# Which engines normalize the fourth group of token blocks: two blocks on VectorE, one on GpSimd and one on ScalarE, in place of four on GpSimd

## The chip, the cores and the metric

The kernel runs on one core of one Trainium2 chip. The metric is device time in microseconds (us) of one execution; the value given is the median of the runs, with the lowest and the highest beside it. A profile is one further execution, recorded instruction by instruction, with a time of its own.

Five engines matter here. TensorE (PE in the profile) multiplies matrices; VectorE (DVE), ScalarE (ACT) and GpSimd (POOL) work elementwise; SyncE (SP) does no arithmetic and issues the transfers (DMA). Each takes its instructions in one fixed order, and an instruction that waits holds up those behind it on its engine.

## The reference

Two branches are computed from the same normalized input and summed with it. The layer norm `xn` of `x` (2048 tokens of 448 channels) comes first:

```
def reference(A_x, A_w_r, A_w_i, B_x, B_w1, B_w2, B_w3, B_w4):
    x = A_x
    xn = _layernorm(x, axis=-1)
    return x + _A_ref(xn, A_w_r, A_w_i) + _B_ref(xn, B_w1, B_w2, B_w3, B_w4)
```

Branch A is a spectral filter: a two-dimensional real FFT, a product with complex weights, and the inverse. Branch B is a mixer:

```
h = _gelu(_layernorm(x, axis=-1) @ w1)
...
hs = jnp.concatenate([g0, g1, g2, g3], axis=-1) @ w2
x1 = x + hs
h2 = _gelu(_layernorm(x1, axis=-1) @ w3) @ w4
return x1 + h2
```

The input of `@ w1` is thus normalized twice. `g0` to `g3` are the four quarters of the channels of `h`, shifted by +1, -1, +2 and -2 tokens.

## The kernel before

**Tiles.** The tokens are cut into 16 blocks of 128 partitions by 448 channels in float32; `xb(b)` is block b, part of a tile `xt`. Neighbouring tokens lie in different blocks, so a shift by tokens is mostly a change of block. Four blocks make a group, and `GRP[3]` is blocks 10, 11, 12 and 13. Values that enter a matmul are split into a high and a low half in float16, and products are made of three matmuls (high by high, low by high, high by low).

**The first stage, group by group.** `norm1(g, apply)` takes the statistics of a group's four blocks on VectorE (L306, L307), makes a first estimate of the reciprocal root (L324 to L327) and the product with the mean (L328, tile `nma`), and then normalizes each block in place: one multiply-add for each block with a scale and a bias for each partition, on the engine that the list `apply` names (L333 on ScalarE, L336 on VectorE or GpSimd). It gives back `refine`, some ten small GpSimd operations (L343 to L352) that finish the root; the last makes `gsc`, the scale that the GELU of that group needs. `scales` (L360 to L367) makes from it the correction `cs` (L365), by which `w2_tile` needs to multiply a block. `refine` and `scales` run on GpSimd alone.

A group then needs its transposed copy `xT`. Groups 0 to 2 are transposed on TensorE (L389) and split by ScalarE and VectorE (L393, L394). Group 3 goes through `turn(3)`: for each block ScalarE copies the high half (L866), VectorE subtracts it twice to get the low half (L867 for 64 channels, L868 for 384), and SyncE issues a transposing DMA (L869).

**`w1_unit(g, i)`** multiplies block i of group g with `w1` (11 matmuls, L420), applies GELU (L460) and writes the high (L461) and low half (L464) into the shift buffer in `x2mem`. When the neighbours of a block are all done, SyncE issues the transposing DMA into `hT`, tile `h` (L475): unit (2,0), block 6, releases block 4. The transposing DMAs of `turn` and those of the units share SyncE's queue.

**`w2_tile(b)`** multiplies `h` of block b with `w2` (11 matmuls, L484) into one of two PSUM banks, and VectorE adds the result to `cs` times the block (L485). With two banks, the third tile cannot begin before the first has been evicted. After L485 come the second layer norm (`ln2`), transposes of its output (L520), and the large multiplications with `w3` (L400) and `w4` (L814), which fill most of the rest of the program. The spectral branch runs between them.

**The order.** The program is not run in source order. A scheduler places the instructions on each engine by priority (by and large the order of the source) and by when it expects their inputs, and the order is then fixed in the program. `behind(key)` holds instructions behind a named earlier one on the same engine. The multiplications of `w3` and `w4` are given a late priority (`FILL`), so that they take what the others leave of TensorE.

The steps around the change, in source order:

Of the kernel before, what the change touches and what calls it, by code (L numbers as in the profile page):

```python
# [125 lines left out]
def body(tc, nc, x, wf, w1, w2, w3, w4, c_g, c_n, c_small, out):  # L126
    V, A, P, T, SY = nc.vector, nc.scalar, nc.gpsimd, nc.tensor, nc.sync
# [40 lines left out]
    def xb(b):  # L168
        return xt[b // 2][:, b % 2]
# [130 lines left out]
    def stats(src, key, mv=None, pins=None):  # L300
        if mv is None:
            mv = pc.tile([128, 4, 2], F32, tag="mv", bufs=3, name=f"mv{key}")
        for i, s in enumerate(src):
            st = pc.tile([128, 6], F32, tag="st", bufs=4, name=f"st{key}_{i}")
            with behind(*pins[i]) if pins else contextlib.nullcontext():
                V.bn_stats(out=st, in_=s)  # L306
            V.bn_aggr(out=mv[:, i, :], in_=st)  # L307
        return mv
# [10 lines left out]
    def norm1(g, apply, pins=None):  # L319

        bs, c = GRP[g], slice(4 * g, 4 * g + 4)
        mv, a, y, nm = mva[:, c], va[:, :, c], vy[:, :, c], nma[:, c]
        stats([xb(b) for b in bs], f"a{g}", mv, pins)
        V.tensor_scalar(out=a[:, 1], in0=mv[:, :, 1], scalar1=1.0 + EPS, scalar2=EPS * EPS, op0=ALU.mult, op1=ALU.add)  # L324
        V.tensor_scalar(out=a[:, 0], in0=mv[:, :, 1], scalar1=EPS, scalar2=None, op0=ALU.add)
        V.tensor_single_scalar(vyi[:, :, c], va.bitcast(I32)[:, :, c], 1, op=ALU.logical_shift_right)
        V.tensor_scalar(out=vyi[:, :, c], in0=vyi[:, :, c], scalar1=-1, scalar2=0x5F3759DF, op0=ALU.mult, op1=ALU.add)  # L327
        i = V.scalar_tensor_tensor(out=nm, in0=mv[:, :, 0], scalar=-1.0, in1=y[:, 1], op0=ALU.mult, op1=ALU.mult)  # L328
        after["c", g] = (i.ins,)
        for k, b in enumerate(bs):  # L330
            y_, m_ = y[:, 1, k:k + 1], nm[:, k:k + 1]
            if apply[k] is A:
                i = A.activation(out=xb(b), in_=xb(b), func=AF.Identity, scale=y_, bias=m_)  # L333
                after["na", g] = (i.ins,)
            else:
                i = apply[k].tensor_scalar(out=xb(b), in0=xb(b), scalar1=y_, scalar2=m_, op0=ALU.mult, op1=ALU.add)  # L336
                after["n" if apply[k] is V else "np", g] = (i.ins,)

        q, z = (pc.tile([128, 2, 4], F32, tag=f"v{t}", bufs=2, name=f"v{t}{g}") for t in "qz")
        w, r = vw[:, :, c], vr[:, :, c]  # L340

        def refine():
            P.tensor_tensor(out=q, in0=y, in1=y, op=ALU.mult)  # L343
            P.tensor_tensor(out=q, in0=q, in1=a, op=ALU.mult)
            P.tensor_scalar(out=w, in0=q, scalar1=-10.0 / 3.0, scalar2=None, op0=ALU.add)
            P.tensor_tensor(out=w, in0=w, in1=q, op=ALU.mult)
            P.tensor_scalar(out=w, in0=w, scalar1=5.0, scalar2=None, op0=ALU.add)
            P.tensor_tensor(out=z, in0=w, in1=w, op=ALU.mult)
            P.tensor_tensor(out=z, in0=z, in1=q, op=ALU.mult)
            P.tensor_scalar(out=z, in0=z, scalar1=-0.5 * 0.375 ** 3, scalar2=1.5 * 0.375, op0=ALU.mult, op1=ALU.add)  # L350
            P.tensor_tensor(out=r, in0=z, in1=w, op=ALU.mult)
            i = P.tensor_scalar(out=gsc[:, c], in0=r[:, 1], scalar1=r1, scalar2=None, op0=ALU.mult)  # L352
            after["g", g] = (i.ins,)
        return refine
# [19 lines left out]
    @contextlib.contextmanager  # L374
    def behind(*key):
        key = key if len(key) > 1 else key[0]
        with contextlib.ExitStack() as st:
            for i in after[key]:
                st.enter_context(tc.issue_after(i))
            yield  # L380
# [501 lines left out]
    n1 = [norm1(0, [P,V,P,V])]  # L882
# [90 lines left out]
    n1[2]()  # L973
    scales(0, 3)
    with behind("a2"):
        n1 = [norm1(3, [P, P, P, P])]
    for k in range(4):
        w1_unit(2, k)
    for k in range(4):
# [166 lines left out]
```

## Time and profile before

| | |
|---|---|
| median of 3 runs | 409.43 us (409.42 to 409.53) |
| profiled execution, its own time | 409.47 us |
| its span (first to last instruction) | 407.7 us |
| TensorE busy | 400.2 us (98%) |
| VectorE busy | 334.7 us (82%) |
| ScalarE busy | 254.1 us (62%) |
| GpSimd busy | 101.0 us (25%) |
| granted TensorE clock, mean | 0.998 |

Times in the profile's rows are us from the start of the span, unless marked ns. A row of a timeline has start, length, engine, line, operation, the tile written and those read (`out<-in`), partitions by elements, and a count; neighbouring instructions of one kind are merged into one row. A bracket at its end says how long the engine stood idle before it and what ended that. A row of a group has the busy time and the mean ns of one, and after the second bar the idle time before the group. A row that lists one line's instructions has their lowest, median and highest length in ns. A row of windows has the stretch, its length, then busy time and count of PE, PEld (weight loads), DVE, ACT and POOL, the granted clock, the busy share of DMA and its GB/s. "SPq" is SyncE issuing a transfer: the length is that of the issue, not of the transfer.

### The profile page before, as it was taken

What the parts mean: (1) busy time and instruction counts of PE and PEld (TensorE: products, weight loads), DVE (VectorE), ACT (ScalarE), POOL (GpSimd) and SP (SyncE); (2) the same over time, 40 slices, a digit from 0 to 9 for tenths busy, and PEclk for the clock granted to TensorE, in tenths of its full rate; (3) what the DMA queues carried; (4) which work ended last, traced back from release to release, by engine and by line L of the source; (5) the groups of instructions that cost most, each with busy time, mean ns of one, the idle gap of its engine ahead of it and who ended that gap; (6) DMA issues with size and microseconds to landing.
All of it is one profiled execution on the core that took longest, in us unless ns stands there. A gap on an engine that the chain in (4) does not pass through costs nothing.

```text
span 407.7 us, 8731 instructions
## 1 busy us (share of the span) xinstructions
PE 400.2 (98%) x3391; PEld 297.6 (73%) x3391; DVE 334.7 (82%) x704; ACT 254.1 (62%) x431; POOL 101.0 (25%) x158
## 2 busy tenths in 40 slices
PE   8999999999999999999999999999999999999995
PEld 3555455865767877777878878787677789998994
DVE  5899799999746897988698888965999999966644
ACT  4787979774468867555698878853354555452431
POOL 6759810111146956500021111110000000000000
PEclk9999999999999999999999999999999999999999
DMA  8978975666759752636256657500012023100101
GB/s 274 382 281 177 247 143 130 135 123 146 182 121 276 238 169 65 221 99 180 73 145 166 153 128 185 131 27 2 24 68 75 20 92 90 47 2 2 45 2 46
DMA packets 54597, 52.08 MB, mean 128 GB/s; under 512 B 35678, under 2 KB 48542, under 8 KB 54556
## 3 DMA queue, kind: packets, MB, share of 16 engines
q1 hardware_dynamic: 54556, 51.53, 46.4%
q8 instruction: 26, 0.43, 0.5%
q14 instruction: 15, 0.12, 0.1%
HBM read 38.28 MB, written 3.67 MB: 103 GB/s over the span
## 4 chain that ended last, share of the span: by engine, by line
PE 89%; POOL 5%; DVE 2%; ACT 1%; issue 1%; DMA 1%; POOLq 0%
PE pw L400 33%; PE acc L814 23%; PE pw L484 6%; PE side L784 4%; PE acc L784 3%; PE pu L673 3%; PE ps L573 3%; PE pe L694 2%; PE pp L628 2%; PE px L645 2%; PE py L715 2%; PE wps L844 2%; PE pw L420 2%; POOL xt L336 1%; POOL w2p L938 1%
## 5 line engine op out<-in xcount | busy, mean ns | idle before, releaser
L400 PE MATMUL pw<-x2mem,w3p 128*128 128x256 f16 x1232 | 151.5, 273 | 0.0
L400 PEld LDWEIGHTS <-w3p 128*128 128x128 f16 x1232 | 119.0, 98 | 19.5
L814 PE MATMUL acc<-w4p,hf 128*128 128x448 f16 (+1 forms) x516 | 104.3, 348 | 0.0
L814 PEld LDWEIGHTS <-hf 128*128 128x128 f16 x516 | 50.1, 98 | 37.6
L732 ACT ACTIVATE pw<-pw,pe 128x512 f32<-128x512 f32 x42 | 27.4, 653 | 27.7 <-PE pw L400 27.6
L735 DVE SCALAR_TENSOR_TENSOR hf<-pw,h,hf 128x512 f16<-128x512 f32 x42 | 31.2, 744 | 12.9 <-ACT hf L734 12.7
L484 PE MATMUL pw<-w2p,h 128*128 128x448 f16 x176 | 36.4, 352 | 1.3 <-DMA h<-x2mem 0.7
L420 PE MATMUL pw<-w1p,xT 128*128 128x448 f16 x176 | 35.0, 352 | 0.0
L654 POOL TENSOR_TENSOR z<-te 128x450 f32<-128x450 f32 x16 | 15.7, 981 | 70.8 <-DVE te L652 65.9
L734 ACT ACTIVATE hf<-pw,h 128x512 f16<-128x512 f32 x42 | 28.8, 686 | 4.2 <-PE acc L814 3.2
L484 PEld LDWEIGHTS <-h 128*128 128x128 f16 x176 | 17.1, 98 | 16.7 <-DMA h<-x2mem 1.7
L750 ACT ACTIVATE hz<-g,h 128x896 f16<-128x896 f32 x14 | 14.6, 1042 | 23.1 <-DVE g L747 23.1
L420 PEld LDWEIGHTS <-xT 128*128 128x128 f16 x176 | 17.1, 99 | 15.8 <-DVE xT L394 0.4
L784 PEld LDWEIGHTS <-hz 128*128 128x128 f16 x294 | 28.3, 98 | 0.6
L635 ACT ACTIVATE pf<-pp 64x450 f16<-64x450 f32 x32 | 17.4, 543 | 12.5 <-DVE pf L636 9.6
L636 DVE TENSOR_TENSOR pf<-pp,pf 64x450 f16<-64x450 f32 x32 | 19.9, 622 | 5.1 <-ACT pf L635 4.8
L751 DVE SCALAR_TENSOR_TENSOR hz<-g,h,hz 128x896 f16<-128x896 f32 x14 | 16.1, 1147 | 6.7 <-ACT hz L750 6.7
L556 POOL TENSOR_TENSOR f<-xr 128x452 f32<-128x452 f32 x16 | 19.7, 1250 | 0.6
L564 DVE TENSOR_TENSOR xh<-f,xh 128x452 f16<-128x452 f32 x16 | 14.3, 915 | 6.2 <-ACT xh L563 6.2
L650 ACT ACTIVATE te<-px 64x450 f32<-64x450 f32 x32 | 17.3, 540 | 1.2 <-PE px L645 0.6
L744 ACT ACTIVATE g<-pw,pe 128x512 f32<-128x512 f32 x14 | 9.6, 683 | 11.3 <-PE pw L400 11.2
L563 ACT ACTIVATE xh<-f 128x452 f16<-128x452 f32 x16 | 8.7, 573 | 9.5 <-POOL f L556 7.8
(189 smaller groups left out, 707.3 us busy)
## 6 DMA issues: line engine op xcount, KB each, us to landing
wc<-wf SPq DMA_DIRECT2D x32, 225.0 KB, 3.8
wl<-wf SPq DMA_DIRECT2D x8, 450.0 KB, 4.1
xt<-x SPq DMA_DIRECT2D x8, 448.0 KB, 7.3
xf<-x SPq DMA_DIRECT2D x8, 448.0 KB, 4.4
loads<-x SPq DMA_DIRECT2D x7, 448.0 KB, 3.9
out<-xt SPq DMA_DIRECT2D x13, 224.0 KB, 1.9
w3raw<-w SPq DMA_DIRECT2D x3, 896.0 KB, 10.9
gn<-c_g SPq DMA_DIRECT2D x16, 128.0 KB, 3.0
```

The lines of the kernel that those rows point to most:

```text
L400: T.matmul(ps_out, wp[:, wi + t, cols], xT[:, xi + t, tok], start=t == 0 and wi + xi == 0, stop=t == 3 and wi == 4)
L420: m = T.matmul(pm[:, :D], xTs[g][:, xi + t, 128 * i:128 * i + 128], w1p[:, wi + t], start=t == 0 and p == 0, stop=t == 3 and p == 2)
L484: T.matmul(pm[:, :D], h[:, k], w2p[:, w], start=n == 0, stop=n == 10)
L556: P.tensor_tensor(out=f[:, :, k:k + 2].rearrange("p b s d -> p s b d"), in0=u[:, :, 0], in1=u[:, :, 1], op=op)
L635: A.activation(out=hi, in_=src, func=AF.Copy)
L636: V.tensor_tensor(out=lo, in0=src, in1=hi, op=ALU.subtract)
L650: A.activation(out=e[64 * h:64 * h + 64], in_=px_[64 - 64 * h:128 - 64 * h, :2 * DF], func=AF.Copy)
L732: A.activation(out=pm, in_=pm, func=AF.Gelu_apprx_tanh, scale=r3)
L734: i = A.activation(out=h[:, 0], in_=pm, func=AF.Copy, scale=h3)
L735: j = V.scalar_tensor_tensor(out=h[:, 1], in0=pm, scalar=h3, in1=h[:, 0], op0=ALU.mult, op1=ALU.subtract)
L784: m = T.matmul(to, h[:, hi, 128 * blk:128 * blk + 128], b[wi], start=new and n == 0, stop=n == 2 and (last if blk in (2, 5, 3, 0) else end ...
L814: m = T.matmul(to, h[:, hi, o:o + 128], w4p[0][:, wi, f, r], start=first and f % 2 == 0 and n == 0, stop=end and f % 2 == 1 and n == 2, sk ...
```

## The change

```
     n1[2]()
     scales(0, 3)
     with behind("a2"):
-        n1 = [norm1(3, [P, P, P, P])]
+        n1 = [norm1(3, [V, P, V, A])]
     for k in range(4):
         w1_unit(2, k)
```

`P`, `V` and `A` stand for GpSimd, VectorE and ScalarE. Block 10 is now normalized by VectorE (L336), block 11 by GpSimd (L336), block 12 by VectorE (L336) and block 13 by ScalarE (L333, an activation with the identity function, the same scale and the same bias). The statistics, `refine`, `scales` and everything after are as before. The engine's own list also decides what `behind("a2")` does to these instructions: on VectorE and ScalarE they are placed behind the copies of group 2's transposes (L394 and L393), on GpSimd it has no effect. The scheduler places all instructions anew.

More of the change, by code (lines that the diff above doesn't have):

```diff
@@ L975, in body @@
     with behind("a2"):
-        n1 = [norm1(3, [P, P, P, P])]
+        n1 = [norm1(3, [V, P, V, A])]
     for k in range(4):
```

## The prediction

> **What bounds the kernel now.** I read the first part of the page first, for the engine that fills the span, then the idle time of that engine by stage, and only then the stretch around the changed line.
>
> ```profile
> span 407.7 us, 8731 instructions
> PE 400.2 (98%) x3391; PEld 297.6 (73%) x3391; DVE 334.7 (82%) x704; ACT 254.1 (62%) x431; POOL 101.0 (25%) x158
> ```
>
> TensorE (PE) is busy 98% of the span. Its matmul groups after 53 us (grouped by line, that window alone) show where it idles:
>
> ```profile
> L400 PE MATMUL pw<-x2mem,w3p 128*128 128x256 f16 x1232 | 151.5, 273 | 0.0
> L814 PE MATMUL acc<-w4p,hf 128*128 128x448 f16 (+1 forms) x516 | 104.3, 348 | 0.0
> L484 PE MATMUL pw<-w2p,h 128*128 128x448 f16 x126 | 25.8, 352 | 0.0
> ```
>
> The last column is idle time before the group, and it is 0.0 for all the large ones. So from 53 us on PE always has work, and a change at 40 us can only pass on what it does to PE before 53 us. The timeline of PE around the changed line:
>
> ```profile
> 39.88 6.22 PE L420 MATMUL pw<-w1p,xT 128*128 128x448 f16 x32
> 46.58 4.32 PE L484 MATMUL pw<-w2p,h 128*128 128x448 f16 x22 [0.49 <-DVE xt L485]
> 51.61 2.25 PE L484 MATMUL pw<-w2p,h 128*128 128x448 f16 x11 [0.71 <-DMA h<-x2mem]
> 53.84 3.00 PE L420 MATMUL pw<-w1p,xT 128*128 128x448 f16 x15
> ```
>
> There are two holes. The bracketed numbers are short, because a matmul's shown end overlaps the next. The chain of waits gives the true pace:
>
> ```profile
> 59.30 2.08 PE pw L484 x11
> ```
>
> That is 2.08 / 11 = 0.189 us for each 448-column matmul. The 32 of the first row fill 39.88 + 32 x 0.189 = 45.93, so hole one is 46.58 - 45.93 = 0.65 us. The 22 of the second fill to 46.58 + 4.16 = 50.74, so hole two is 51.61 - 50.74 = 0.87 us. Together they are **1.52 us**, the most that this change can gain while the later stages stay full.
>
> **What makes the holes.** Hole one is named by its releaser, the eviction L485 on VectorE (DVE), which waits for `cs`, and `cs` is made on GpSimd (POOL) between the four block normalizations:
>
> ```profile
> 40.80 0.71 POOL L336 TENSOR_SCALAR xt<-xt,vy,nma 128x448 f32<-128x448 f32 x1
> 41.47 0.21 POOL L366 TENSOR_TENSOR nm<-mva,vw 128x12 f32<-128x12 f32 x1
> 41.67 1.78 POOL L336 TENSOR_SCALAR xt<-xt,vy,nma 128x448 f32<-128x448 f32 x2
> 43.42 0.20 POOL L363 TENSOR_TENSOR cs<-cs,vw 128x12 f32<-128x12 f32 x1
> 43.61 1.01 POOL L336 TENSOR_SCALAR xt<-xt,vy,nma 128x448 f32<-128x448 f32 x1
> 45.49 0.32 POOL L365 TENSOR_SCALAR cs<-cs,s 128x12 f32<-128x12 f32 x1
> ...
> 39.85 0.19 DVE L328 SCALAR_TENSOR_TENSOR nma<-mva,vy 128x4 f32<-128x4 f32 x1
> 42.15 0.30 DVE L867 TENSOR_TENSOR x<-xt,x 128x64 f16<-128x64 f32 x1 [2.10 <-ACT x L866]
> 43.96 0.80 DVE L464 SCALAR_TENSOR_TENSOR x2mem<-pw,h,x2mem 128x224 f16<-128x224 f32 x2
> 45.85 1.27 DVE L485 SCALAR_TENSOR_TENSOR xt<-xt,cs,pw 128x448 f32<-128x448 f32 x2 [1.09 <-POOL cs L365]
> ```
>
> Hole two waits for a transfer. SyncE's queue (SP) issues `h` of block 4 (L475), which needs the low half that DVE writes at 43.96 to 44.76. Its issue begins at 48.09 all the same, because two transfers of `turn` (L869) stand before it:
>
> ```profile
> 43.09 4.89 SPq L869 DMA_TRANSPOSE xT<-x  x2
> 48.09 1.53 SPq L475 DMA_TRANSPOSE h<-x2mem  x1
> 49.72 2.58 SPq L869 DMA_TRANSPOSE xT<-x  x2
> ...
> 48.09 3.48 DMA h<-x2mem
> ```
>
> The last row, of the chain, has it landing at 51.57; PE starts at 51.61. The first L869 in turn starts when block 10 has been normalized by POOL, copied by ScalarE (ACT) and subtracted by DVE:
>
> ```profile
> 41.54 0.58 ACT L866 ACTIVATE x<-xt 128x448 f16<-128x448 f32 x1 [3.33 <-POOL xt L336]
> 42.02 0.59 ACT L460 ACTIVATE pw<-pw,gsc 128x448 f32<-128x448 f32 x1
> ```
>
> ACT waits 3.33 us and DVE 2.10 us there. Both engines have room just where the change puts work.
>
> **The change, part by part.** Blocks 10 and 12 go to DVE, 11 stays on POOL, 13 goes to ACT. No wait, buffer or transfer is added; what moves is order. Prices on the new engines come from the same operation on other groups:
>
> ```profile
> L336 DVE TENSOR_SCALAR xt<-xt,vy,nma x5: 506/511/833, 8.1 to 28.6; 128x448 f32<-128x448 f32 x5
> L333 ACT ACTIVATE xt<-xt,nma,vy x2: 750/756/761, 18.2 to 29.2; 128x448 f32<-128x448 f32 x2
> ```
>
> *POOL loses three blocks.* Its four take 40.80 to 41.47, 41.67 to 43.42 and 43.61 to 44.59 = 0.67 + 1.75 + 0.98 = 3.40 us; one stays at 0.7 to 1.0, so `cs` comes 2.4 to 2.7 us sooner, near 43.3 in place of 45.81. L485 then runs before 45.2, and hole one needs only 0.65 us of that: **-0.65 us** at PE's arrival at hole two.
>
> *DVE gains two blocks,* 2 x 0.51 = 1.02 us, at most 2 x 0.83 = 1.67, from 40.04 on, where it stood idle for 2.10 us. What follows is L867 of block 10, which the copies on ACT release. Cost nothing; with the cover gone it would be 1.0 to 1.7 us on DVE alone, which L485's 2.5 us of new slack still holds.
>
> The trace has one DVE block at 833 ns against the usual 511, and POOL blocks from 0.71 to about 1 us. [...]
>
> *ACT gains one block,* 0.75 us at about 40.06, inside its 3.33 us of idle. Behind it wait the first L866 and, after that, L460 of unit (2,0). The copy of block 10 starts at 40.06 + 0.75 = 40.81 in place of 41.54, or near 40.6 if the copy goes ahead of the block.
>
> *SP's first L869* came 43.09 - 41.54 = 1.55 us after its L866 began. From 40.81 that makes 42.36, from 40.6 it makes 42.15: **0.73 to 0.94 us earlier**. If L475 keeps the third place and each issue keeps its length, `h` lands by as much sooner, at 50.6 to 50.8. PE arrives at 50.74 - 0.65 = 50.09 and still waits 0.6 us or so.
>
> So with PE's order kept, the gain is SP's advance, 0.73 to 0.94, not the sum of the holes. The order on each engine isn't the source's, however (POOL runs L363 between two blocks of a line that stands elsewhere), and it is made anew for the changed kernel. With group 3's `xT` on its way earlier, matmuls of its unit (L420), which run now from 53.84, may be placed ahead of block 4's L484; they would fill the hole, and the gain goes to 1.52. I take **-1.0 us**, between 0.73 and 1.52 and nearer to the queue's row, because the second needs a new order. The bounds of this part are 0 (below) and -1.52.
>
> *Sum.* Span 407.7 - 1.0 = 406.7. The profiled execution took 409.47, 1.77 outside its span; the median of the runs shown is 409.43, 0.04 below it. Forecast: 409.43 - 1.0 = **408.4 us**.
>
> **The rivals.**
>
> *The loads hold the transfer (no change).* While the two L869 are issued, DMA is full, and it nearly stops before the transposes flow:
>
> ```profile
> 42.50:47.25 4.75, 4.26 (x23) 2.15 (x22) 3.46 (x8) 4.75 (x10) 4.24 (x14) 1.00 1.00 305
> 47.50:48.75 1.25, 1.25 (x8) 0.68 (x7) 1.25 (x5) 1.25 (x2) 1.20 (x4) 1.00 0.91 37
> 49.00:52.00 3.00, 2.29 (x13) 0.99 (x11) 3.00 (x11) 3.00 (x8) 1.73 (x5) 1.00 1.17 261
> ...
> w4half<-w SPq DMA_DIRECT2D x1, 1344.0 KB, 10.6
> ```
>
> The columns at the end are DMA share and GB/s: 305, then 37, then 261. The 1344 KB load is issued before 40 us and lands 10.6 us later. If the two L869 are so slow to issue (4.89 us, against 2.58 for the next two) because that load is ahead of them, a start at 42.4 only waits longer, `h` lands at 51.57 again, and hole two swallows hole one whole: 409.4. For it: 4.89 against 2.58. Against it: nothing shows which of the two, queue or load, ends last. [...]
>
> *L475 falls back in SP's queue (slower).* All four blocks of `turn` are now ready at about the same time, near 41 us, where POOL dealt them out over 3.4 us; so a third or fourth L869 can be placed ahead of L475 of block 4. Each costs 2.58 / 2 = 1.29 us of queue. One place: 1.29 - 0.73 = +0.6 us, 410.0; two places: 2.58 - 0.73 = +1.85, 411.3. With the load holding the queue, the 0.73 isn't taken off: 410.7 and 412.0. It decides as soon as one more L869 stands ahead and PE keeps its order; with the matmuls of group 3 placed ahead of block 4's, it wouldn't. For it: L869 stands ahead of L475 twice already. Against it: ACT still has unit (2,0)'s L460 second, and DVE has the two L485 to do before the later blocks, which holds those back.
>
> *A worse order later.* PE has no idle time after 53 us, while DVE and ACT are full just there:
>
> ```profile
> 60.00:70.00 10.00, 10.00 (x55) 5.17 (x53) 10.00 (x15) 10.00 (x15) 0.00 (x0) 1.00 0.61 151
> ```
>
> An order with other neighbours there can open a new hole in PE; by the two that exist, 0.65 to 0.87 us each: 410.1 to 411.2 for one or two. For it: DVE and ACT at 10.00 of 10.00. Against it: both enter that stretch with work done earlier.
>
> *The change does nothing where it counts.* If `cs` is not brought forward, because the planned order puts other POOL work into the freed time, hole one stays and so does the time, 409.4. POOL has only operations of 0.2 to 0.3 us left there, so I hold it with the first rival.
>
> **How the numbers follow.** Forecast (holes shrink, -0.7 to -1.5) 0.45; the loads hold the transfer, or nothing is moved 0.20; L475 falls back 0.24; a worse order later 0.11. 0.2% of 409.43 is 0.82 us, about what a measurement of this kernel can tell from no change. Of the forecast's 0.45, some 0.05 lies under 0.82: faster 0.40. Within: 0.20 less a little, plus 0.05, and 0.04 for one place lost at +0.6: same 0.25. Slower: 0.35. The forecast's own range is 407.9 to 408.7. The range for 8 in 10 goes from 407.9 (all of both holes) up past the two lost places and the two new holes: 411.3.
>
> **What would show it.** In the changed profile's page and timelines: POOL has one L336 after 40 us, DVE two and ACT one L333; `cs` (L365) ends near 43.3; the first L869 starts at 42.2 to 42.4; L484's x22 row has no idle before it. Then the place of L475 in SP's queue and its landing decide: 50.7 by the forecast, 51.6 by the load, 52.4 or later if it fell back. L420 between L484's x22 and the next x11 would show the full 1.52. The forecast is wrong if PE's hole before block 4 is as long as 0.87 + 0.65, or if PE has idle time after 53 us that it didn't have.

## The result and the profile after

| | before | after |
|---|---|---|
| median of 4 runs | 409.48 us (409.42 to 410.08) | 413.04 us (412.42 to 413.78) |
| ratio, 95% interval | | 1.0084 (1.0065 to 1.0104) |
| profiled execution, its own time | 409.47 us | 413.78 us |
| its span | 407.7 us | 412.1 us |
| granted TensorE clock, mean | 0.998 | 0.991 |

The changed kernel is 3.56 us slower. The forecast was 408.4 us with a range to 411.3, so the change went the other way and the time lies outside the range. From the page after:

```profile
PE 402.4 (98%) x3391; PEld 298.3 (72%) x3391; DVE 337.0 (82%) x706; ACT 255.1 (62%) x432; POOL 99.4 (24%) x155
...
PEclk9999969999999999999999999999999999999999
...
L484 PE MATMUL pw<-w2p,h 128*128 128x448 f16 x176 | 38.3, 367 | 3.9 <-DMA h<-x2mem 3.8
```

The work moved as the change says: POOL has three instructions fewer, DVE two more, ACT one more. PE has the same 3391 matmuls. The digit 6 in the clock row (slice 6, 51.5 to 61.8 us) was a 9 before, and the L484 group has 3.9 us of idle before it, nearly all of it a wait for `h`. Both lie in the same place. The timeline of SP, after:

```profile
42.50 8.33 SPq L869 DMA_TRANSPOSE xT<-x  x4
50.93 5.27 SPq L475 DMA_TRANSPOSE h<-x2mem  x4
```

And that of PE, after:

```profile
39.84 6.22 PE L420 MATMUL pw<-w1p,xT 128*128 128x448 f16 x32
45.89 4.33 PE L484 MATMUL pw<-w2p,h 128*128 128x448 f16 x22
54.02 4.29 PE L484 MATMUL pw<-w2p,h 128*128 128x448 f16 x11 [3.81 <-DMA h<-x2mem]
```

All four transposes of `turn` (L869) now stand ahead of the transfer of block 4's `h` (L475): it fell from the third place to the fifth, and its issue from 48.09 to 50.93. The x22 row has no idle before it: hole one is closed. It fills to 45.89 + 4.16 = 50.05, and PE starts again at 54.02, so hole two is 3.97 us where it was 0.87. Then the 11 matmuls of block 4 take 4.29 us where they took 2.25. The reason stands in the windows (the third number from the end is the granted clock):

```profile
50.00:53.20 3.20, 0.21 (x2) 0.00 (x0) 3.20 (x15) 2.61 (x6) 0.04 (x1) 1.00 1.00 214
53.20:60.00 6.80, 5.98 (x18) 2.82 (x19) 2.37 (x13) 1.34 (x3) 0.86 (x2) 0.50 0.55 104
62.00:130.00 68.00, 68.00 (x453) 44.18 (x452) 58.94 (x139) 47.59 (x77) 11.02 (x19) 1.00 0.67 148
```

The same two stretches in the kernel before:

```profile
53.20:60.00 6.80, 6.80 (x39) 3.68 (x38) 6.76 (x37) 4.49 (x9) 0.86 (x2) 1.00 0.61 119
62.00:130.00 68.00, 68.00 (x465) 45.37 (x464) 57.94 (x133) 47.87 (x78) 14.54 (x23) 1.00 0.67 150
```

From 53.2 to 60.0 the granted clock is 0.50; before, the same 6.8 us were at 1.00 with 39 matmuls in place of 18. From 62 us on both kernels keep PE busy throughout. The chain of waits, after, confirms the transfer and gives the last row of PE:

```profile
50.93 3.05 DMA h<-x2mem
54.02 4.29 PE pw L484 x11
...
404.17 4.58 PE acc L814 x36
```

The same row, before:

```profile
398.82 4.58 PE acc L814 x36
```

PE thus ends 5.35 us later. Worked out: the holes together grew from 1.52 to 3.97 us, +2.45. Half speed from 54.02 to 60.0 loses 5.98 x 0.5 = 2.99. The sum is 5.44. The span grew by less, 4.4 us, because from the start of that row to the end of the span 8.88 us passed before and 7.93 after; what shortened this end isn't known. This profiled execution is also the slowest of the four: the other three have mean clocks of 0.994 to 0.995 in place of 0.991, which agrees with a shorter stretch at half speed, and the median is +3.56.

### The profile page after: what moved, and what is told of

Its sections match the earlier page's. It is cut to its first block, busy times and chain, and to the rows that moved or that the text cites. A ratio compares the mean times of both kernels' runs of the same rounds, so it can differ in the third digit from the quotient of the medians.

```text
span 412.1 us, 8730 instructions
## 1 busy us (share of the span) xinstructions
PE 402.4 (98%) x3391; PEld 298.3 (72%) x3391; DVE 337.0 (82%) x706; ACT 255.1 (62%) x432; POOL 99.4 (24%) x155
## 4 chain that ended last, share of the span: by engine, by line
PE 86%; POOL 4%; DVE 3%; DMA 3%; ACT 2%; issue 1%; SPq 1%; ACTq 0%
PE pw L400 33%; PE acc L814 23%; PE pw L484 7%; PE side L784 4%; PE acc L784 3%; PE pu L673 3%; PE ps L573 3%; PE pe L694 2%; PE pp L628 2%; PE px L645 2%; PE pw L420 2%; PE py L715 2%; DMA w1s<-w 1%; POOL w2p L938 1%; DMA h<-x2mem 1%
## 5 line engine op out<-in xcount | busy, mean ns | idle before, releaser
L400 PE MATMUL pw<-x2mem,w3p 128*128 128x256 f16 x1232 | 151.6, 273 | 0.0
L400 PEld LDWEIGHTS <-w3p 128*128 128x128 f16 x1232 | 119.0, 98 | 19.5
L484 PE MATMUL pw<-w2p,h 128*128 128x448 f16 x176 | 38.3, 367 | 3.9 <-DMA h<-x2mem 3.8
L420 PE MATMUL pw<-w1p,xT 128*128 128x448 f16 x176 | 35.9, 358 | 0.0
L484 PEld LDWEIGHTS <-h 128*128 128x128 f16 x176 | 17.6, 101 | 20.7 <-DMA h<-x2mem 4.8
L420 PEld LDWEIGHTS <-xT 128*128 128x128 f16 x176 | 17.5, 101 | 16.4 <-issue 0.9
L485 DVE SCALAR_TENSOR_TENSOR xt<-xt,cs,pw 128x448 f32<-128x448 f32 x16 | 10.7, 672 | 7.0 <-PE pw L484 6.2
```

The costliest lines, as they stand in the source:

```text
L400: T.matmul(ps_out, wp[:, wi + t, cols], xT[:, xi + t, tok], start=t == 0 and wi + xi == 0, stop=t == 3 and wi == 4)
L420: m = T.matmul(pm[:, :D], xTs[g][:, xi + t, 128 * i:128 * i + 128], w1p[:, wi + t], start=t == 0 and p == 0, stop=t == 3 and p == 2)
L484: T.matmul(pm[:, :D], h[:, k], w2p[:, w], start=n == 0, stop=n == 10)
```

## The experiments

Theory: the time is set by the place of block 4's `h` in SyncE's queue and by the half clock that follows a long hole; the new division of the blocks by itself gains about what was forecast. Rival A: the division itself costs time (GpSimd and VectorE in each other's way, or a worse order later). Rival B: the big load sets when `h` lands, whatever its place. Each batch ran on one chip beside the kernel before, whose median there was 409.09 us (first four kernels below), 409.2 (the next four) and 409.41 (the last four). The ratios are against that.

| kernel | place of block 4's `h` | issue | PE starts on it | PE's wait | time, us | ratio (95%) |
|---|---|---|---|---|---|---|
| q3_third | third | 48.24 | 51.80 | 1.39 | 408.49 | 0.9987 (0.9978 to 0.9997) |
| q4_fourth | fourth | 50.08 | 53.17 | 2.69 | 410.67 | 1.0047 (1.0029 to 1.0064) |
| q2_second | second | 47.48 | 50.92 | 0.63 | 407.83 | 0.9974 (0.9965 to 0.9984) |
| b_late | fifth or later | | 57.45 | none | 410.01 | 1.0027 (1.0015 to 1.0039) |
| fill | fifth | 50.85 | 53.93 | filled | 411.31 | 1.0058 (1.0036 to 1.0079) |
| b5_late | sixth | 52.21 | 55.37 | 4.11 | 415.19 | 1.0148 (1.013 to 1.0166) |
| b2_second | second | 45.36 | in a row of 33 | about 0.1 | 408.91 | 0.9995 (0.9983 to 1.0007) |
| q2_early | second | 46.05 | 51.48 | 0.72 | 408.86 | 0.9992 (0.9981 to 1.0002) |
| q1_first | first | 47.65 | 50.68 | 0.22 | 407.57 | 0.9955 (0.994 to 0.997) |
| one_block | third | 48.25 | 51.80 | 1.08 | 408.96 | 0.9992 (0.9981 to 1.0003) |
| two_blocks | fourth | 49.50 | 52.59 | 2.24 | 410.7 | 1.0037 (1.0022 to 1.0051) |
| change_again | fifth | 51.12 | 54.20 | 3.93 | 413.06 | 1.009 (1.0069 to 1.011) |

The wait is from the end of the L484 row before it (its start plus 0.189 us for each matmul) to the start of block 4's; for b5_late and q2_early it is the bracket of the row. In b2_second and q1_first the rows before and after block 4's start are merged into one of 33 matmuls: q1_first's start is taken from the chain, and b2_second's wait is the 6.53 us of its row less the 6.41 that 33 take without a wait (4.33 for 22, and 11 x 0.189).

**The place alone, with the new division.** One line holds the last of `turn`'s issues behind that of block 4's `h`; nothing is added or left out. Four kernels differ in the bound: 3, 2, 1 and 0. With 3 and 2, PE, DVE, ACT and POOL have the changed kernel's order line by line in the trace, and only SP's differs; with 1 and 0 a few more differ (14 and 20 places of PE's 3391).

```
         for i, b in enumerate(GRP[g]):
...
-            d = SY.dma_start_transpose(...)
+            with behind("h", 2, 0) if i >= 2 else contextlib.nullcontext(): d = SY.dma_start_transpose(...)
```

Bound 2, the third place that the forecast had assumed:

> The change kept; only the issues of turn's last two blocks (L869) are held behind the issue of h for block 4 (L475), so that this one is third in SyncE's queue as it was before the change. TensorE, VectorE, ScalarE and GpSimd keep the changed kernel's order instruction by instruction. If the place in the queue makes the loss: h lands near 51.3, the hole in TensorE before block 4 falls from 3.97 us to about 1.3, the granted clock stays 1.00 after it, and the time is 409.2 to 409.8. If the other engines' new order (499 rows of difference on TensorE, 255 on VectorE) makes it: 412 to 414, as the change has. If the queue's earlier start is worth what the prediction took: 408.4.

SP's timeline of q3_third:

```profile
42.79 5.35 SPq L869 DMA_TRANSPOSE xT<-x  x2
48.24 2.86 SPq L475 DMA_TRANSPOSE h<-x2mem  x2
```

PE's timeline of q3_third at block 4:

```profile
51.80 2.25 PE L484 MATMUL pw<-w2p,h 128*128 128x448 f16 x11 [1.23 <-DMA h<-x2mem]
```

The transfer in its chain of waits:

```profile
48.24 3.51 DMA h<-x2mem
```

And its window of 54 to 58 us, the stretch in which the changed kernel had half clock:

```profile
54.00:58.00 4.00, 4.00 (x25) 2.08 (x23) 3.27 (x19) 2.64 (x6) 0.88 (x2) 1.00 0.80 160
```

Only SP's order differs from the changed kernel. The 3.56 us of loss are gone, and 0.6 us are gained (interval 0.12 to 0.90). Rival A falls: the division doesn't cost time. The clock stays at 1.00. But the forecast's way to a gain isn't here either: `h` lands at 48.24 + 3.51 = 51.75, no sooner than before (51.57), and PE's holes are 1.39 us in place of 1.52. The 0.13 us between them lies just inside the interval; where more of the 0.6 us would come from isn't shown.

Bound 3, the fourth place:

> The change kept; only the issue of turn's last block is held behind that of h for block 4, which is then fourth in the queue. The other engines keep the changed kernel's order. By the queue, h lands one issue (1.33 us) sooner than with the change, 52.6, and the hole is 2.6 us. If a hole of that length lets the granted clock fall to 0.5 as 3.97 us did: 411 to 412.5; if not: 410.2 to 410.7.

PE's timeline of q4_fourth at block 4:

```profile
53.17 3.30 PE L484 MATMUL pw<-w2p,h 128*128 128x448 f16 x11 [2.53 <-DMA h<-x2mem]
```

And a window of it, where the granted clock is the number after POOL:

```profile
54.20:57.60 3.40, 3.40 (x12) 1.66 (x11) 1.27 (x8) 0.78 (x2) 0.86 (x2) 0.50 0.89 179
```

The clock fell here too, for 3.4 us, after a hole of 2.69. The eight runs stand in two heaps: 409.6 to 410.36 with mean clocks of 0.998 to 1.0, and 410.99 to 412.05 with 0.995 to 0.996. The mean of the first heap (409.92) is 1.43 us above q3_third, as its hole is longer by 1.30; the second (411.62) lies another 1.70 above it, and 3.4 us at half speed lose 1.7.

Bound 1, the second place, and bound 0, all four L869 behind block 4's `h`:

> The change kept; turn's last three issues are held behind that of h for block 4, which is then second. The issue has to wait for the low half of unit (2,0), written until 47.57 in the changed kernel, so by the queue it gains little over the third place: h lands near 50.7, the hole is 0.7 us, 408.6 to 409.2. If the load before the transposes sets the landing, 51.3 and 409.2 to 409.8.

> The change kept; all four of turn's issues held behind that of h for block 4, which is then first in the queue after the loads. It has to wait for the low half until 47.5, and turn's transposes only after it. If the landing near 50.9 in q2_second came from the transpose issued before it: h lands 3.0 us after its issue, near 50.5, hole 0.2 us, 0.3 us below q2_second, 407.5. If the load ahead or the data set it: 50.9 again and 407.8. If group 3's transposes, now 5 us later, are missed by its matmuls: above 409.

At the second place PE still waits 0.63 us. At the first, 0.22; SP's timeline of q1_first:

```profile
47.65 1.24 SPq L475 DMA_TRANSPOSE h<-x2mem  x1
```

PE's timeline of q1_first:

```profile
46.30 6.64 PE L484 MATMUL pw<-w2p,h 128*128 128x448 f16 x33
```

The chain of waits of q1_first, at block 4 and at its end:

```profile
47.65 2.99 DMA h<-x2mem
50.68 2.26 PE pw L484 x11
...
397.99 4.59 PE acc L814 x36
```

Hole one is gone, and hole two is down to 50.68 - (46.30 + 4.16) = 0.22 us, so 1.30 of the 1.52 us are closed. PE's last row starts 0.83 us sooner than in the kernel before. At 407.57 us, 0.9955 of it (1.2 to 2.5 us less by the interval), q1_first is the fastest of all and beats both kernels. Along the places from first to fifth the times are 407.57, 407.83, 408.49, 410.67 and 413.04, against 409.09 to 409.48 for the kernel before on their chips.

**The place alone, with the old division.** If the place is the cause, the kernel before must lose by it too. b_late takes the issue of block 4's `h` out of `w1_unit` and makes it after `turn(3)`; the four blocks stay on GpSimd:

```
+            issue = lambda b=b: SY.dma_start_transpose(...).ins
+            after["h", g, i] = held.append(issue) if (g, i) == (2, 0) else (issue(),)
...
-    n1[0]()
+    with behind("t", 3): held[0](); n1[0]()
```

> The kernel before the change (GpSimd normalizes all four blocks); only the issue of h for block 4 is moved behind all four of turn's, fifth in the queue. If the place alone makes the loss: h lands near 54.2, the hole is 3.5 us, the granted clock falls, and the time is 412 to 414 without the change. If the division of the four blocks makes it: 409.5.

PE's timeline of b_late, its rows before and after block 4, and one much later:

```profile
51.41 6.21 PE L420 MATMUL pw<-w1p,xT 128*128 128x448 f16 x32
57.45 4.33 PE L484 MATMUL pw<-w2p,h 128*128 128x448 f16 x22
...
116.42 0.93 PE L814 MATMUL acc<-w4p,hf 128*128 128x448 f16 x4 [0.66 <-ACT hf L734]
```

This missed. The scheduler saw the late `h` and placed 32 matmuls of group 3 (L420) ahead of block 4, so no hole opened and the clock stayed at 1.00. The +0.9 us came from waits of PE later, 0.66 us at 116.4 us the longest. So it says nothing on what a late place costs when PE has to wait, but it shows that for a late `h` an order existed in which PE doesn't wait for it. b5_late takes that way out as well, by holding group 3's L420 behind block 4's last L484:

```
-        w1_unit(3, k)
+        with behind("w2t", 4): w1_unit(3, k)
```

> The kernel before the change with h for block 4 fifth in SyncE's queue, as in b_late, and the matmuls of group 3 (L420) held behind those of block 4 on TensorE, so that they can't fill the hole. If the place in the queue, and not the division of the blocks among engines, makes the loss: h lands at 54.2, a hole of 3.4 us, granted clock 0.5 after it, 411.5 to 413. If the division makes it: 409 to 410.

PE's timeline of b5_late:

```profile
55.37 5.62 PE L484 MATMUL pw<-w2p,h 128*128 128x448 f16 x22 [4.11 <-DMA h<-x2mem]
```

The transfer in its chain of waits:

```profile
52.21 3.11 DMA h<-x2mem
```

The issue that PE waits for even came sixth, and the old division lost 1.48%: a hole of 4.11 us, and a clock of 0.50 for 3.4 us. The loss needs no block on another engine. The converse, `h` pulled up to second place in the kernel before (the line above with `i >= 1` and `[P, P, P, P]`):

> The kernel before the change; only turn's last three issues are held behind h for block 4, which is then second in place of third. The other four engines keep the order of before. Its data are ready at 44.8, so the issue can begin near 45.2. By the queue h lands about 1.3 us sooner, near 50.3, and hole two (0.87 us) closes while hole one stays: 0.9 us less than before. If the load ahead sets the landing: no change.

PE's timeline of b2_second:

```profile
46.81 6.53 PE L484 MATMUL pw<-w2p,h 128*128 128x448 f16 x33 [0.49 <-DVE xt L485]
```

Hole two is nearly gone, hole one (GpSimd's `cs`) stays, and the time can't be told from that of before (-0.05%, interval -0.17% to +0.07%). The expected 0.9 us did not come; the last PE row (398.56) is only 0.26 us earlier. Of the 0.75 us that the hole lost, 0.23 was gone before it in this execution (the row starts at 46.81, 46.58 before). Where the rest went stays open, and no gain from closing hole two alone is shown.

**The hole without the half clock.** fill adds 16 matmuls into block 4's bank, whose result block 4's first matmul overwrites; they keep PE busy while it waits:

```
-        pm = bank("sp", f"pw2_{b}")
+        pm = bank("sp", f"pw2_{b}"); [T.matmul(pm, wsrc[:, 0:128], wsrc, start=True, stop=True) for _ in range(16 if b == 4 else 0)]
```

> The change kept, with 16 matmuls on constants (216 ns each, 3.46 us; their results are overwritten) put into the PSUM bank of block 4 ahead of its own eleven, where TensorE idled 3.97 us. The transfer isn't touched, h lands at 54 as with the change. If the idle time itself lets the granted clock fall to 0.5 and that costs the 2.9 us seen after the hole: the clock stays 1.00 and the time is 413.04 - 2.9 = 410.1, though TensorE is given more work. If the clock falls for another reason, or the slow matmuls aren't the clock's: 412.5 to 413.5.

PE's timeline of fill:

```profile
50.02 2.97 PE L481 MATMUL pw<-wsrc 128*128 128x512 f16 x13
...
53.93 4.33 PE L484 MATMUL pw<-w2p,h 128*128 128x448 f16 x22 [0.16 <-DMA h<-x2mem]
```

Its window of 54 to 58 us:

```profile
54.00:58.00 4.00, 4.00 (x22) 2.08 (x23) 3.96 (x21) 3.83 (x7) 0.77 (x2) 1.00 0.88 167
```

`h` lands as late as in the changed kernel (53.93 against 54.02), PE did 16 matmuls more, and the clock is 1.00. The last PE row starts at 400.99 against 404.17: 3.18 us sooner, where the half clock was worked out to lose 2.99. So in this execution the clock follows PE's idle time, not the late transfer. The whole runs gain less: fill is 2.11 us above the kernel before on its chip, the change 3.56 on its own, so 1.45, and one of four still has a clock of 0.995 (412.59 us); the insertion also changes the order behind it. The size is therefore shown by the trace of one execution and in part by the times.

**What sets the landing.** q2_early is q2_second with ScalarE's and VectorE's part of `turn` for the last three blocks held behind unit (2,0) too (`with behind(2, 0) if i >= 1` ahead of L866 to L868), so that its L464 and the issue come sooner:

> The change kept, h for block 4 second in the queue as in q2_second, and the copies and subtractions of turn's last three blocks held behind unit (2,0) on ScalarE and VectorE, so that the low half is written some 1.5 to 2 us earlier than 47.5. If the data's lateness is what q2_second still waits for: the hole before block 4 (0.65 us) closes, 0.5 us less than q2_second. If the load ahead sets the landing: the same as q2_second.

SP's timeline of q2_early:

```profile
46.05 2.62 SPq L475 DMA_TRANSPOSE h<-x2mem  x1
```

PE's timeline of q2_early:

```profile
51.48 2.25 PE L484 MATMUL pw<-w2p,h 128*128 128x448 f16 x11 [0.72 <-DMA h<-x2mem]
```

And a window of it between the load and the transposes:

```profile
48.00:49.50 1.50, 1.50 (x10) 0.77 (x9) 1.50 (x8) 1.50 (x3) 0.77 (x2) 1.00 1.49 72
```

The last number is what DMA moved, 72 GB/s. This missed: issued 1.43 us sooner than in q2_second (47.48), `h` was there 0.56 us later (51.48 against 50.92). Issued at 47.48 or later, it lands 3.0 to 3.5 us after its issue in all runs; issued at 46.05 (q2_early) or 45.36 (b2_second), it needs 5.4 and 5.5. In no run is it there before 50.6 us. What the landing goes by shows when it is counted from the issue of the 1344 KB load (L238). SP's row of that issue, in the kernel before and in the changed one (it starts at 38.89 in q3_third and 38.86 in one_block):

```profile
38.66 0.59 SPq L238 DMA_DIRECT2D w4half<-w  x1
...
38.62 0.59 SPq L238 DMA_DIRECT2D w4half<-w  x1
```

From the start of that row to PE's start on block 4's `h`, at the third place, it is 12.95 us before, 12.91 in q3_third and 12.94 in one_block (below), although the first L869 was issued 4.43, 3.90 and 3.75 us after the load. At the other places it is 11.64 (first), 12.06 (second, q2_second; 12.28 in q2_early), 13.99 and 14.06 (fourth), 15.37 to 15.40 (fifth) and 16.78 (sixth). In one_block the low half of unit (2,0) was written at 45.43 already (L464), so its data didn't hold the issue of 48.25 either. So rival B holds in part: counted from the load, the landing goes by the place in the queue, and an earlier start of `turn`'s transposes brings nothing. That isn't what moved the time between the kernels, since the load is the same in all and the place differs; but it takes away the advance of the queue on which the forecast's gain rested. No run here moves the load, so that it is the load, and not something else of that time, is not shown. (q2_early's time says little: its PE waits 0.5 us more later on, at L400.)

**How much of the division brings it about.** One block moved (`[V, P, P, P]`), then two (`[V, P, V, P]`), no order held:

> Only block 10 goes to VectorE, blocks 11 to 13 stay on GpSimd; no pins. The built order has h for block 4 third in SyncE's queue, as before. If the place decides: no long hole, clock 1.00, and hole one shorter by one block of GpSimd (0.9 us, more than its 0.65), so between before and q3_third: ratio 0.997 to 1.000. If taking blocks off GpSimd is bad in itself, a quarter of the changed kernel's loss: ratio 1.002.

> Blocks 10 and 12 go to VectorE, 11 and 13 stay on GpSimd; no pins. The built order has h for block 4 fourth in the queue. If the place decides: as q4_fourth, a hole of 2.5 to 2.7 us, ratio 1.002 to 1.007, the runs in two heaps according to whether the clock falls. If ScalarE's block 13 is what hurts: no hole, ratio below 1.001.

SP's timeline of one_block:

```profile
42.61 5.54 SPq L869 DMA_TRANSPOSE xT<-x  x2
48.25 1.53 SPq L475 DMA_TRANSPOSE h<-x2mem  x1
```

And of two_blocks:

```profile
42.46 6.95 SPq L869 DMA_TRANSPOSE xT<-x  x3
49.50 1.25 SPq L475 DMA_TRANSPOSE h<-x2mem  x1
```

With one block off GpSimd, `h` stays third; with two it is fourth, with three (the change) fifth. The time follows the place and not the division: 408.96, 410.7 and 413.04 us here, against 408.49 and 410.67 for the full division held to the third and fourth place.

**The change again,** on the last chip:

> The changed kernel as it is, on the same chip as these. Fifth place, h lands 3.0 us after its issue at 50.9, a hole near 4.0 us. The clock falls in every run, for 3.4 or 6.8 us by the records so far (3.4 in q4_fourth and b5_late, 6.8 in the changed kernel's profile), which is 1.7 or 3.4 us of TensorE: 411.5 to 414, ratio 1.006 to 1.010.

It gave 413.06 us, with a wait of 3.93 us and, in the profiled execution (412.53), half clock for 3.4 us (53.9 to 57.3). Two lengths of half clock thus occur in one kernel. Its four runs lie at 412.53, 412.85, 413.27 and 413.72 us with mean clocks of 0.996, 0.995, 0.994 and 0.991.

## Why the prediction was wrong, point by point

**GpSimd loses three blocks: right in kind, mis-sized.** POOL's timeline, after:

```profile
41.20 0.75 POOL L336 TENSOR_SCALAR xt<-xt,vy,nma 128x448 f32<-128x448 f32 x1
41.92 0.50 POOL L366 TENSOR_TENSOR nm<-mva,vw 128x12 f32<-128x12 f32 x1
...
43.16 0.56 POOL L367 TENSOR_SCALAR nm<-nm 128x12 f32<-128x12 f32 x1
...
44.09 0.31 POOL L365 TENSOR_SCALAR cs<-cs,s 128x12 f32<-128x12 f32 x1
```

`cs` ended at 44.40, 1.4 us sooner, where 2.4 to 2.7 were forecast. The block starts 0.4 us later than before, and two small operations take 0.50 (L366) and 0.56 (L367) in place of 0.21 and 0.25, while VectorE subtracts (L868, 41.45 to 42.36 and 43.07 to 43.62). L363 at 42.38, also beside a subtraction, took 0.20 as it did before, so what lengthened the other two isn't shown. The lengthening cost nothing that counts: the slack was larger, and hole one closed.

**VectorE and ScalarE gain blocks in idle time: right.** ACT's timeline, after:

```profile
40.00 0.76 ACT L333 ACTIVATE xt<-xt,nma,vy 128x448 f32<-128x448 f32 x1 [1.83 <-DVE nma L328]
40.67 1.96 ACT L866 ACTIVATE x<-xt 128x448 f16<-128x448 f32 x4
42.53 1.14 ACT L460 ACTIVATE pw<-pw,gsc 128x448 f32<-128x448 f32 x2
```

DVE's timeline, after:

```profile
40.00 0.99 DVE L336 TENSOR_SCALAR xt<-xt,vy,nma 128x448 f32<-128x448 f32 x2
...
43.07 0.55 DVE L868 TENSOR_TENSOR x<-xt,x 128x384 f16<-128x384 f32 x1
44.44 1.27 DVE L485 SCALAR_TENSOR_TENSOR xt<-xt,cs,pw 128x448 f32<-128x448 f32 x2 [0.82 <-POOL cs L365]
45.63 0.22 DVE L867 TENSOR_TENSOR x<-xt,x 128x64 f16<-128x64 f32 x1
45.76 0.55 DVE L868 TENSOR_TENSOR x<-xt,x 128x384 f16<-128x384 f32 x1
...
46.77 0.80 DVE L464 SCALAR_TENSOR_TENSOR x2mem<-pw,h,x2mem 128x224 f16<-128x224 f32 x2
```

The two blocks took 0.99 us (1.02 forecast) and the one 0.76 (0.75), in time that had been idle. The first L869 was issued at 42.50, 0.59 us sooner (0.73 to 0.94 forecast).

**The step that failed: "If L475 keeps the third place and each issue keeps its length, `h` lands by as much sooner".** Neither condition held, and the conclusion fails even where the place is kept. The argument against the rival was that ACT had L460 of unit (2,0) second and DVE had the two L485 to do, which would hold the later blocks back. The rows show the reverse. ACT does all four copies (L866) in one row and L460 after them. DVE does three pairs of subtractions before the L485, the fourth pair after them, and only then L464 of unit (2,0), at 46.77 in place of 43.96. It was not the later blocks that were held back but the unit: with its input made 2.81 us later and four L869 ready, L475 came fifth. The order of before had been read as if the freed engines would keep it, though the text itself had said that it is made anew. The traces show the order; that early readiness made the scheduler choose it is inferred from them and from the row of one, two and three blocks moved. The second condition failed as well. With the third place kept, the first L869 came, counted from the load's issue, 0.53 us (q3_third) and 0.68 (one_block) sooner than before, but the first two took 5.35 and 5.54 us in place of 4.89, and PE started on `h` 12.91 and 12.94 us after the load in place of 12.95. Of the advance of 0.73 to 0.94 us, on which the gain of 1.0 us rested, 0.01 to 0.04 came through: at that place the landing stayed as the first rival had it, though that the load held it isn't shown.

**The rival that came true was priced too low.** Two places lost were put at +1.85 us (411.3). The landing did come later by 53.98 - 51.57 = 2.41 us, against 1.85: the four L869 take 8.33 us, 4.89 + 2.58 = 7.47 before, which is more than their start 0.59 us sooner brought. The prediction's other figure for the same case, 2.58 us with the load holding the queue (412.0), comes near it. With PE arriving 0.69 us sooner at hole two, its hole grew by 3.10. What had no price at all was the half clock, 2.99 us of PE in the profiled execution. The page before shows the clock at 9 of 10 or more throughout, with a longest hole of 0.87 us here. The forecast asked how long PE would wait, and never what follows a long wait.

**The other rivals.** What "The loads hold the transfer" foretold came true together with the lost place, and not in its stead: the advance was lost as it says, and the place made the loss. "A worse order later" did not occur: PE has no more idle time after the hole than before. With the third place, q3_third's 408.49 us stand beside the forecast of 408.4, but that is luck: the kernel before had 409.09 on that chip, so the gain is 0.6 and not 1.0, and the holes closed by only 0.13 us. What was right is that closing both holes pays: q1_first closed 1.30 of the 1.52 us, and the 1.30 lies inside the interval of its gain (1.84 us by the medians, 407.57 against 409.41).

## What to carry to other kernels

Where an engine issues transfers in a fixed order, making the inputs of some ready sooner can put them ahead of the one that the critical engine waits for (here it fell from the third place to the fifth, its issue from 48.09 to 50.93): after any move of work, read that queue's order first, and hold the urgent transfer ahead of the others by hand. The move and the hold together gained 0.45%; the move alone lost 0.84%. Before counting on an earlier issue, ask what else sets the landing: here three different starts of the queue (3.75, 3.90 and 4.43 us after the load ahead) gave the same landing (12.91 to 12.95 us after it). Price a hole in TensorE of 2.24 us or more, the shortest here whose runs show a lower clock, at more than its length: after the 2.69 us of q4_fourth, the runs whose clock fell took another 1.70 us on average.

## What the runs showed of the hardware

- **Half clock after a hole.** With waits of up to 1.39 us the clock stayed at 1.00 in the profiles. At 2.24 us (two_blocks) it stayed in the profiled run, but four of the ten runs have mean clocks of 0.994 to 0.996 and 411.54 to 412.15 us, against 409.69 to 410.85 for the others. At 2.69 (q4_fourth) it was four of eight; at 3.93 and 3.97 (the change) all eight, and at 4.11 (b5_late) all four. In the four profiles that show it, the granted clock was 0.50 for 3.4 us three times (q4_fourth, b5_late, change_again) and for 6.8 once (the changed kernel). What sets these lengths, and what a wait between 1.39 and 2.24 us does, isn't shown.
- **A transposing transfer behind a large load.** Issued at 46.05 us, behind the 1344 KB load of 39.20 (q2_early), its issue takes 2.62 us and its landing 5.4; issued at 47.65 (q1_first), 1.24 and 3.0. At one place in the queue PE could start on it 12.91 to 12.95 us after the issue of the load, whether the first transpose was issued 3.75 or 4.43 us after the load.
